# A written list of 1453 jobs in another order: linear attention, then a gated feed-forward block, on one core

## The chip, the core and the metric

The kernel runs on one core of one Trainium2 chip. It is written for the engines directly: TensorE (PE in the profile, with its weight loads as PEld), VectorE (DVE), ScalarE (ACT), GpSimd (POOL) and SyncE (SP). Each engine takes its own instructions strictly in the order in which the program issues them. SyncE does nothing but start DMAs here; GpSimd starts the loads from memory and most stores. The metric is the time of one execution on the device, in microseconds (us).

## What is computed

Inputs are q, k and v (8 batches, 8 heads, 576 positions, 64 values a head) and three weight matrices. First comes linear attention with position weights, then a feed-forward block over the 4608 tokens:

```python
r = np.maximum(x, 0.0); phi = concat([r * cos_w, r * sin_w])      # x = q, k
kv = einsum('bhsf,bhsd->bhfd', phi(k), v);  z = sum(phi(k), axis=2)
num = phi(q) @ kv;  den = phi(q) . z + 1e-6
x = (num / den)                        # 4608 tokens x 512
g = x @ w_gate;  val = x @ w_val       # 512 -> 1536
out = (silu(g) * val) @ w_out          # 1536 -> 512
```

The output is 4608 x 512 in float32.

## The kernel before, in words

The 4608 tokens are 36 tiles of 128, taken in nine groups of four tiles (group 0 to 8, `tg` in the code; a tile is `t`, a batch is `b`, and a batch has four and a half tiles). The kernel keeps three kinds of work going at once: attention for coming tiles, the two wide products of the current group, and the output product of the group before.

**Attention.** For each batch, GpSimd loads k, v and q (`load_job`, lines 120 and 125). ScalarE and VectorE make the features of q (`feature_jobs`, L880 to L890, into `r_q`), and SyncE transposes them by one DMA (L852, `phit<-r_q`). TensorE makes the key-value sums of a batch in 72 products of 64 rows (`kv_job`, L718); four copies bring them to memory (L630, tile `kv`). A tile's products (`tile_jobs`, L784 and L789) read both; then come the denominators (L803), the reciprocal (L809) and the multiplication to x (L817, L820). From tile 8 on SyncE turns x by a DMA (`turn_job`, L749, `xT<-x`); tiles 4 to 7 are turned by TensorE (L757) and copied by ScalarE (L630). For tiles 4 to 8 the features are turned by TensorE as well (`turned_tiles`, L1323), with a relu (L280, L282) and a multiplication (L1339).

**The wide products.** Group 0 and part of the value products are plain products of 512 columns (L440, L917, L1065). The rest goes through a scheme with seven products of half size, M1 to M7, in place of eight (`block_jobs`, L990), of 256 columns each, with sums of x (`x_sum_jobs`, L963) and of weights (L501) made ahead, and with copies and additions between the products (L630 on ScalarE, L1010, L1018 and L1026 on VectorE). A SiLU (L1049) and a multiplication (L1085) follow, and the result lies in `ht`.

**The output product** has the same scheme, P1 to P7 (`out_jobs`, L1155), with sums of `ht` (L1106), additions (L1198, L1212) and copies to the output buffer (L632, L636). Two output buffers take turns. Stores of group 0 go out on SyncE (L1124), those of groups 1 to 6 and half of group 7 on GpSimd, the other half of group 7 on SyncE. The last group uses buffers of its own, works in halves and stores in pieces on SyncE and ScalarE (L1253 for two tiles, L1262 for one).

**What sets the order.** All this work after the first 26.9 us is cut into 1453 jobs: one job is one instruction of VectorE or ScalarE, or the four to 72 products that belong together. A job knows what it must come after. At the end of the function stands `ORDER`, a list written out by number. The loop below it takes the words one after another and issues each job to its engine; so the list fixes, for every engine, the order of its instructions. A word is the job's number, then `a` or `v` where a job can run on either engine and is given to ScalarE or VectorE, and after a colon the numbers of the PSUM banks or buffer slots that the job takes:

```python
for word in ORDER.split():
    n, e, at = re.match(r"(\d+)([av]?):?([\d,]*)", word).groups()
    j, at = jobs[int(n)], [int(x) for x in (at.split(",") if "," in at else at)]
    j.eng = {"a": "ACT", "v": "DVE", "": next(iter(j.engs))}[e]
```

An engine whose next instruction isn't ready waits, and all that is listed behind it on that engine waits too, ready or not.

The numbers that matter below:

| jobs | what they are |
|---|---|
| 34; 35 to 38 | key-value job of batch 1; its four copies |
| 67, 84, 101 | turned features of tiles 4 and 5, 6 and 7, 8; relus 68, 70, 85, 87, 102 |
| 72, 78, 89, 95, 104 | products of tiles 4 to 8; their turns on TensorE (tiles 4 to 7) 76, 82, 93, 99; the copies of the turned x 77, 83, 94, 100 |
| 113 to 123; 124 | features of batch 2 (113 and 114 on VectorE, 115 to 123 on ScalarE); their transpose on SyncE |
| 55, 58, 61, 64; 56, 57, 59, 60, 62, 63, 65, 66 | copies of group 0's output; its stores |
| 182 to 185; 197, 199 | the four x sums of group 1; its products M7 and M6 that read 182 and 184 |
| 106, 107; 108 | tile 8's reciprocal and multiplication; its transpose |
| 142, 147, 152; 146, 151, 156 | products of tiles 9, 10, 11; the transposes of their x |
| 138; 139 to 141 | GpSimd's wait for tile 8's transpose; three loads behind it |
| 348; 354 | the first x sum of group 2; the product that reads it |
| 468 to 471, 474 to 477; 656; 657 | stores of group 2; GpSimd's wait for batch 4's features; a load |
| 523; 635; 710 | key-value job of batch 5; a copy of group 3's output to a buffer; a product of group 4 |
| 1307; 1309 to 1312 | the last product of group 7; the stores behind it on SyncE |
| 1422 and 1423; 1424 and 1425; 1427; 1431 and 1432 | last group: P6 in halves; the additions behind it; second part of P2; P5 in halves |
| 1410, 1414 | last group: two sums of `ht` for P3 |
| 1429, 1435; 1441, 1443, 1449, 1451 | last group: SyncE's stores of two tiles; its stores of one tile |

Of the kernel before, what the change touches and what calls it, by code (L numbers as in the profile page):

```python
# [18 lines left out]
def kernel(  # L19
# [1403 lines left out]
    for tg in range(1, NTG):  # L1423
# [43 lines left out]
        6:7 4:6 12:1 8:0 10:5 16:3 20:4 29 5:8 9:7 13:0 17:1 1:3 376 7 187 28 191 11 186 188 189 31 30 24:7 18:2 26:3  # L1467
        22:6 21:6 25:2 33 32 2:7 67:0 34:45 14:1 70a 36a 35a 38a 37a 3 27 380 19 68v 69 15 23 71 0 41:2 44 40:0 43
        72:340 84:7 78:561 39:1 42 73 74 75:3 85a 79 86 80 87v 81:2 88 76:3 77 45 101:7 89:560 95:341 47 90 96 377
        102a 378 91 92:3 97 48 82:5 93:6 55:1 83 94 98:0 192 193 109 190 103 110 113 381 114 46 99:1 51:3 52 49  # L1470
# [105 lines left out]
```

## Time and profile before

| | |
|---|---|
| three runs | 298.09, 299.3 and 299.79 us, median 299.3 |
| profiled execution | 298.66 us |
| its span, first to last instruction | 296.8 us |
| granted TensorE clock, mean | 0.996 |
| instructions | 8157, of them 3292 matmuls |
| DMA | 40.90 MB, mean 138 GB/s over the span |

The profile is of one execution, by the hardware's profiler. Its page gives the busy time of each engine, groups of instructions by line of the code with the mean duration of one and the idle time before them, and the chain of work that ended last. The trace behind it answers by stretch, by tile and by time. Matmuls overlap and their ends are modelled: the step from one product's start to the next one's says more than the length of either. A DMA's row on its queue is the time of its issue; when it landed is given apart.

### The profile page before, as it was taken

How to read it: one execution, taken by the hardware profiler on the slowest of the kernel's cores; microseconds unless marked ns; L12 is line 12 of the kernel's file. 1: busy time of each engine (PE TensorE's matmuls, PEld its weight loads, DVE VectorE, ACT ScalarE, POOL GpSimd, SP SyncE). 2: the span in 40 equal slices, each digit the busy share in tenths (PEclk: the TensorE clock that was granted, in tenths of full speed). 3: DMA queues.
4: the chain of work that ended last, by engine and by line, in shares of the span. 5: the costliest groups of instructions: out<-in, count | busy, mean ns of one | idle time of the engine just before them, and what ended most of it. 6: DMA issues, size and time to landing. Idle time of an engine off the chain costs nothing.

```text
span 296.8 us, 8157 instructions
## 1 busy us (share of the span) xinstructions
PE 290.1 (98%) x3292; PEld 237.7 (80%) x3292; DVE 252.9 (85%) x513; ACT 199.1 (67%) x423; POOL 69.1 (23%) x122
## 2 busy tenths in 40 slices
PE   8999999999999999999999999999999999999993
PEld 4697455665877888988898898888988898888882
DVE  7976889889987899999898977998778968968882
ACT  6664347978479868985499689976566555564630
POOL 7963530012015012213343020400050032002000
PEclk9999999999999999999999999999999999999998
DMA  7999999999969999599959947980270036000226
GB/s 255 232 196 198 202 206 209 229 202 155 170 149 171 199 209 144 102 172 148 209 118 159 197 68 131 208 146 2 38 171 8 2 89 127 0 2 18 55 53 161
DMA packets 71973, 40.90 MB, mean 138 GB/s; under 512 B 48768, under 2 KB 68736, under 8 KB 71936
## 3 DMA queue, kind: packets, MB, share of 16 engines
q0 software_dynamic: 24800, 24.39, 49.9%
q1 hardware_dynamic: 46528, 15.47, 27.6%
q10 hardware_dynamic: 608, 0.52, 0.6%
q8 instruction: 26, 0.43, 0.6%
q14 instruction: 11, 0.09, 0.1%
HBM read 37.75 MB, written 9.44 MB: 159 GB/s over the span
## 4 chain that ended last, share of the span: by engine, by line
PE 87%; DMA 9%; DVE 2%; issue 0%; DVEq 0%
PE banks L990 43%; PE banks L1155 23%; DMA xT<-x 4%; DMA phit<-r_q 4%; PE banks L440 4%; PE banks L917 4%; PE banks L1275 3%; PE banks L789 3%; PE banks L718 2%; PE banks L1065 2%; DMA wo_sb<-in_v_dram 1%; DVE v L292 1%; PE banks L371 1%; PE banks L784 1%; PE banks L1323 0%; PE banks L314 0%
## 5 line engine op out<-in xcount | busy, mean ns | idle before, releaser
L1124 POOL DMA_DIRECT2D out_dram<-ob x52 | 27.3, 532 | 128.4 <-ACT ob L632 87.6
L630 ACT COPY banks<-banks 128x512 f32<-128x512 f32 (+1 forms) x53 | 30.4, 577 | 22.3 <-PE banks L990 9.9
L1049 ACT ACTIVATE sg<-banks 128x512 bf16<-128x512 f32 x72 | 40.9, 599 | 5.8 <-PE banks L990 5.6
L1085 DVE TENSOR_TENSOR ht<-sg,banks 128x512 f16<-128x512 bf16 x60 | 40.4, 682 | 4.8 <-PE banks L990 4.4
L1155 PEld LDWEIGHTS <-ht 128*128 128x128 f16 x384 | 37.5, 98 | 4.5
L990 PEld LDWEIGHTS <-wg_sb 128*128 128x128 f16 x384 | 36.7, 98 | 5.3
L990 PEld LDWEIGHTS <-wgs_sb 128*128 128x128 f16 x368 | 35.4, 98 | 6.4 <-issue 0.5
L1010 DVE TENSOR_TENSOR banks<-m,banks 128x512 f32<-128x512 f32 x44 | 30.2, 692 | 7.3 <-PE banks L990 6.0
L990 PEld LDWEIGHTS <-wv_sb 128*128 128x128 f16 x320 | 31.2, 98 | 3.7
L990 PE MATMUL banks<-kvt,wgs_sb 128*128 128x256 f16 x236 | 33.8, 273 | 0.3 <-DVE kvt L963 0.3
L1155 PEld LDWEIGHTS <-sums 128*128 128x128 f16 x288 | 28.0, 98 | 3.4
L630 ACT COPY m<-banks 128x512 f32<-128x512 f32 x44 | 25.5, 590 | 5.7 <-PE banks L990 5.7
L990 PE MATMUL banks<-xT,wg_sb 128*128 128x256 f16 x192 | 28.6, 273 | 0.0
L632 ACT ACTIVATE ob<-banks 128x512 f32<-128x512 f32 x32 | 19.1, 596 | 10.6 <-PE banks L1155 9.3
L1155 PE MATMUL banks<-wo_sb,ht 128*128 128x256 f16 x192 | 25.2, 273 | 0.0
L990 PE MATMUL banks<-kvt,wg_sb 128*128 128x256 f16 x168 | 24.4, 273 | 0.0
L1155 PE MATMUL banks<-wt_sb,sums 128*128 128x256 f16 x192 | 24.2, 273 | 0.0
L820 DVE TENSOR_TENSOR x<-banks,rec 128x512 f16<-128x512 f32 x31 | 21.3, 690 | 3.1 <-PE banks L990 0.5
L990 PE MATMUL banks<-xT,wv_sb 128*128 128x256 f16 x160 | 23.8, 273 | 0.0
L1155 PE MATMUL banks<-wt_sb,ht 128*128 128x256 f16 x192 | 22.8, 272 | 0.0
L890 ACT ACTIVATE r_q<-raw_q,tanq 128x256 bf16<-128x256 bf16 x45 | 20.1, 507 | 0.0
L292 DVE TENSOR_TENSOR v<-raw_kv,tab 128x1152 bf16<-128x1152 bf16 x27 | 19.9, 750 | 0.0
(160 smaller groups left out, 540.1 us busy)
## 6 DMA issues: line engine op xcount, KB each, us to landing
out_dram<-ob POOLq DMA_DIRECT2D x52, 128.0 KB, 3.3
raw_kv<-in_k_dram POOLq DMA_DIRECT2D x7, 576.0 KB, 6.2
raw_q<-in_q_dram POOLq DMA_DIRECT2D x12, 288.0 KB, 9.9
raw_kv<-in_v_dram POOLq DMA_DIRECT2D x6, 576.0 KB, 9.3
out_dram<-ob SPq DMA_DIRECT2D x12, 128.0 KB, 2.8
wg_sb<-in_moe_w_gate_dram POOLq DMA_DIRECT2D x5, 256.0 KB, 9.0
wv_sb<-in_moe_w_val_dram POOLq DMA_DIRECT2D x5, 256.0 KB, 9.6
wo_sb<-in_v_dram SPq DMA_DIRECT2D x2, 576.0 KB, 4.1
```

The costliest lines, as they stand in the source:

```text
L292: nc.vector.tensor_tensor(out=v2s[b == 1][:, g, :, :, 0:D], in0=(first if b == 0 and g == 0 else {"v": raw_of(b, "v")})["v"][:, g].unsquee ...
L440: nc.tensor.matmul(out=st["f", tg, fc, lo][i], lhsT=(wg_sb, wv_sb)[i][:, kc, fs], rhs=xT[tg][:, ts, kc], start=(kc == 0), stop=(kc == KC - 1))
L630: nc.scalar.copy(out=out, in_=in_)
L632: nc.scalar.mul(out=out, in_=in_, mul=mul)
L820: tt(out=x_.rearrange("p (i y d) -> p i y d" if pairs else "p (y e d) -> p e y d", d=D, **({"i": 2} if pairs else {"e": 2})), in0=view()[: ...
L890: nc.scalar.activation(out=home()[:, :, c, 1], in_=raws[b, "q"][:, :, c], func=AF.Relu, scale=tanq[:, c:c + 1])
L990: nc.tensor.matmul(out=to[:, i], lhsT=a[:, c, 2 * u + i], rhs=x()[:, :, c], start=first and i == 0 and c == 0, stop=c == KH - 1, skip_grou ...
L1010: tt(out=bank(c), in0=one(m7_all, m).rearrange("p i x -> p (i x)"), in1=bank(b), op=ALU.add)
L1049: nc.scalar.activation(out=gates(rooms[w])[:, :, jh * HT:(jh + 1) * HT], in_=src, func=AF.Silu, scale=DOWN)
L1085: tt(out=ht[:, 4 * u + w:4 * u + w + 3:2, jh * HT:(jh + 1) * HT], in0=gates(rooms[w])[:, :, jh * HT:(jh + 1) * HT], in1=src.rearrange("p ( ...
L1124: {"POOL": nc.gpsimd, "SP": nc.sync, "ACT": nc.scalar}[j.eng].dma_start(out=out_v[idx // NC, idx % NC][:, cols], in_=ob_of(t)[e * SH:(e + ...
L1155: nc.tensor.matmul(out=to, lhsT=a[:, kc, i * P:(i + 1) * P], rhs=b[:, kc], start=first and kc == 0 and i == 0, stop=kc == HC - 1, skip_gro ...
```

## The change

`ORDER` is replaced by another list of the same jobs. Each job occurs once in both. TensorE's order differs in 379 of 490 places, GpSimd's in 51 of 74, SyncE's in 22 of 52; on VectorE and ScalarE nearly all places differ by some steps. 353 words name other banks or slots. Jobs 35, 37, 70, 85 and 102 go from ScalarE to VectorE, 68 and 87 from VectorE to ScalarE. No other line of the kernel changes. The parts of both lists that the text speaks of, shortened:

```diff
-        6:7 4:6 12:1 8:0 10:5 16:3 20:4 29 5:8 9:7 13:0 17:1 1:3 376 7 187 28 191 11 186 188 189 31 30 24:7 18:2 26:3
-        22:6 21:6 25:2 33 32 2:7 67:0 34:45 14:1 70a 36a 35a 38a 37a 3 27 380 19 68v 69 15 23 71 0 41:2 44 40:0 43
-        72:340 84:7 78:561 39:1 42 73 74 75:3 85a 79 86 80 87v 81:2 88 76:3 77 45 101:7 89:560 95:341 47 90 96 377
...
-        104:451 195:7 50 100 122 118 120 123 58 116 117 119 115 121 105 196:0 57 59 56 60 124 382 182 183 184 185 106
-        107:3 218:1 53 197:6 54 199 61:0 198:0 200:2 194 132 220:5 214:4 202 203 128 126 130 64 219:6 125 221:2 131
...
-        1424:1 1425:2 1430 1431 1432 1433 1434 1437 1438 1435 1436 1439 1445 1442 1440 1446 1444 1447 1441 1443 1449
-        1450 1448 1451 1452
+        4:2 8:5 6:4 10:3 12:0 5:2 9:1 13:0 376 7 1:3 11 187 20:4 16:6 24:7 14:1 2:5 22:3 26:2 21:8 29 25:3 188 189 191
+        30 31 3 33 32 28 0 27 15 67:7 34:45 40:1 39:0 42 18:2 68a 69 186 35v 37v 70v 23 71 36a 17:7 38a 19 377 84:5
+        78:341 72:670 43 41:2 44 79 87a 73 85v 80 380 378 86 74 81:0 75:1 47 45 89:341 101:5 76:6 90 88 91 92:3 102v
...
+        52 53 54 94 123 116 117 121 119 118 122 115 120 100 105 58 61:0 196:1 56 124 183 182 106 107:2 184 185 132
...
+        1418:1 1391 1411 1406 1426 1308 1412 1309 1420 1413 1427 1310 1421:0 1410 1422 1311 1428:1 1414 1423 1312
+        1424:4 1430 1431 1429 1425:5 1432 1433 1437 1434 1438 1435 1436 1439 1445 1441 1442 1440 1446 1443 1444 1447
+        1449 1450 1448 1451 1452
```

SyncE's first jobs are 57 59 56 60 124 108 63 66 65 62 146 156 151 168 in the old list and 56 124 108 62 60 57 146 65 59 63 66 156 151 168 in the new one. GpSimd's jobs around 656 are 656 477 475 657 501 658 471 502 in the old list and 656 474 476 475 471 477 657 501 658 502 in the new one.

More of the change, by code (lines that the diff above doesn't have):

```diff
@@ L1466 @@
     ORDER = """
-        6:7 4:6 12:1 8:0 10:5 16:3 20:4 29 5:8 9:7 13:0 17:1 1:3 376 7 187 28 191 11 186 188 189 31 30 24:7 18:2 26:3
-        22:6 21:6 25:2 33 32 2:7 67:0 34:45 14:1 70a 36a 35a 38a 37a 3 27 380 19 68v 69 15 23 71 0 41:2 44 40:0 43
-        72:340 84:7 78:561 39:1 42 73 74 75:3 85a 79 86 80 87v 81:2 88 76:3 77 45 101:7 89:560 95:341 47 90 96 377
-        102a 378 91 92:3 97 48 82:5 93:6 55:1 83 94 98:0 192 193 109 190 103 110 113 381 114 46 99:1 51:3 52 49
[63 rows of a table removed]
+        4:2 8:5 6:4 10:3 12:0 5:2 9:1 13:0 376 7 1:3 11 187 20:4 16:6 24:7 14:1 2:5 22:3 26:2 21:8 29 25:3 188 189 191
+        30 31 3 33 32 28 0 27 15 67:7 34:45 40:1 39:0 42 18:2 68a 69 186 35v 37v 70v 23 71 36a 17:7 38a 19 377 84:5
+        78:341 72:670 43 41:2 44 79 87a 73 85v 80 380 378 86 74 81:0 75:1 47 45 89:341 101:5 76:6 90 88 91 92:3 102v
[64 rows of a table added]
     """
```

119 rows, old and new, of the table ORDER are left out of this document.

## The prediction

> **What bounds the kernel now.** I read the head of the page first, then the busy time by stretch, then the chain of waits with each engine's timeline at the two places where TensorE stands still.
>
> ```profile
> span 296.8 us, 8157 instructions
> PE 290.1 (98%) x3292; PEld 237.7 (80%) x3292; DVE 252.9 (85%) x513; ACT 199.1 (67%) x423; POOL 69.1 (23%) x122
> ```
>
> TensorE is busy for 98% of the span. That is no proof of a full engine, so the next view cuts the span at the two places without work (columns: stretch; its length; busy us and count of PE, weight loads, VectorE, ScalarE, GpSimd; clock; DMA).
>
> ```profile
> 26.88:63.80 36.92, 36.92 (x463) 21.44 (x461) 31.59 (x69) 24.42 (x53) 8.31 (x12) 1.00 1.28 213
> 63.80:64.80 1.00, 0.68 (x8) 0.37 (x6) 1.00 (x2) 1.00 (x2) 0.00 (x0) 1.00 0.19 26
> 64.80:82.00 17.20, 17.20 (x144) 12.43 (x145) 15.59 (x30) 11.46 (x26) 2.92 (x5) 1.00 1.13 169
> 82.00:82.60 0.60, 0.27 (x4) 0.09 (x2) 0.50 (x2) 0.00 (x0) 0.00 (x0) 1.00 1.27 289
> 82.60:291.85 209.25, 209.25 (x2352) 184.73 (x2351) 181.80 (x345) 146.31 (x309) 39.13 (x73) 1.00 0.62 111
> 291.85:296.80 4.95, 0.00 (x1) 0.00 (x0) 0.42 (x1) 0.00 (x0) 0.00 (x0) 0.79 0.61 158
> ```
>
> The list of jobs begins at 26.88 us. From there to 291.85, which is 265.0 us, TensorE is idle for 0.32 and 0.33 us, at a clock of 1.00. The steps from product to product say whether it is also full (first the chain of waits: start, length, count; then TensorE's timeline at the first gap):
>
> ```profile
> 27.05 9.50 PE banks L917 x44
> 137.04 1.17 PE banks L718 x68
> 152.25 12.23 PE banks L990 x112
> 241.18 15.28 PE banks L990 x140
> ```
>
> ```profile
> 63.87 0.60 PE L990 MATMUL banks<-kvt,wg_sb 128*128 128x256 f16 x4
> 64.78 0.69 PE L789 MATMUL banks<-kv,phit 128*128 128x65 bf16 x16 [0.32 <-DMA phit<-r_q]
> ```
>
> A product of 256 columns steps by 12.23 / 112 = 0.109 us early and 15.28 / 140 = 0.109 late, one of 512 by 9.50 / 44 = 0.216. The code has 1232 + 672 of the first kind (L990, L1155) and 160 of the second after 26.88: 1904 x 0.1092 + 160 x 0.216 = 242.5 us. The seven key-value jobs at 1.17, and the small products of tiles and turns, take most of the other 22.5. So the list runs at TensorE's own pace, and **the same jobs in any order hold at least about 264 us of it.** An order can give back only waits. Start to start, the first wait is 64.78 - 63.87 - 4 x 0.109 = 0.47 us, since a modelled end (0.60 for four steps of 0.109) hides 0.16 of it; the second, by the same, 0.33 + 0.16 = 0.49. What the sum leaves beside them is no idle time. I take it as fixed: the new list goes over to tile products 27 times, the old one 24 times.
>
> **The change, part by part.** Both lists hold the same 1453 jobs: 490 of TensorE, 74 of GpSimd, 52 of SyncE. Nothing is computed anew; order, banks and slots change, and seven jobs change engine. I call the *place* of a product 26.88 plus the steps of all products listed ahead of it. With work this dense, it says when TensorE gets there, apart from waits.
>
> *1. The transpose of batch 2's features (124), and tile 9 (142) that waits for it.*
>
> ```profile
> 53.56 11.17 DMA phit<-r_q
> 47.84 1.63 ACT L630 COPY xT<-banks 128x512 f16<-128x512 f16 x3
> 49.36 1.70 ACT L890 ACTIVATE r_q<-raw_q,tanq 128x256 bf16<-128x256 bf16 x4
> 50.97 0.58 ACT L632 ACTIVATE ob<-banks 128x512 f32<-128x512 f32 x1
> 51.45 2.09 ACT L890 ACTIVATE r_q<-raw_q,tanq 128x256 bf16<-128x256 bf16 x5
> ```
>
> Before, ScalarE does three copies of turned x (83, 94, 100), four features, a copy out (58) and five features, and 124 leaves at 53.56. The new list puts all nine features straight behind the second copy, which ended at 48.9: nine at 0.42 (1.70 / 4, 2.09 / 5) end at 52.7, and 124 leaves 0.9 us earlier. Three of the four stores that SyncE issued just ahead of it go behind it. At 11.17 it lands at 63.9. Tile 9's place is 63.39, against 63.81 before; with 0.5 lost by then, as before (64.78 less the wait of 0.5 against 63.81), it is due at 63.9: the wait goes. **-0.5** (from -0.5 to 0). What is late next is the third copy.
>
> *2. The third copy (100), and the x sums of group 1 (182 to 185).*
>
> ```profile
> 53.47 0.60 PE L990 MATMUL banks<-kvt,wgs_sb 128*128 128x256 f16 x4
> 52.00 0.75 DVE L963 TENSOR_TENSOR kvt<-xT 128x512 f16<-128x512 f16 x2
> 53.72 0.20 DVE L809 RECIPROCAL rec<-den 128x8 f32<-128x8 f32 x1
> 54.03 0.76 DVE L817 TENSOR_TENSOR x<-banks,rec 128x256 f16<-128x256 f32 x2
> ```
>
> Copy 100 now starts at 52.7 and ends at 53.2 (1.63 / 3 = 0.54 each), where it ended at 49.5. The first two sums need it and end at 53.2 + 0.75 = 53.95. Their product (197, the first row) started 0.39 behind its place of 53.08; its new place is 53.51, so it is due at 53.9: it just fits. Behind them VectorE now has tile 8's reciprocal and multiplication (0.20 + 0.76), then the sum for product 199: ready at about 55.45, due at 54.82 + 0.4 = 55.2. **+0.3** (0 to 0.8).
>
> *3. The transposes of x tiles 11 and 10 (156, 151), and the sums of group 2 behind them (348).*
>
> ```profile
> 61.33 1.19 SPq L749 DMA_TRANSPOSE xT<-x  x1
> 62.63 3.33 SPq L1124 DMA_DIRECT2D out_dram<-ob  x4
> 66.91 6.35 SPq L749 DMA_TRANSPOSE xT<-x  x3
> 69.92 12.09 DMA xT<-x
> 82.10 0.44 DVE kvt L963
> DVE kvt L963 <- DMA xT<-x: 1.0, 1, 1.0
> DMA to landing us min/median/max: 11.9/12.8/13.8
> ```
>
> Before, SyncE issues four stores ahead of the three transposes; the new list puts three stores ahead of the first and four more between it and the other two. The last row is of the q loads that GpSimd issues at 67.2 to 67.9: 13.8 later, at 81.7, the last lands, and the transposes land at 82.0. Both end when the shared traffic ends. The four stores (3.33) make 156 and 151 leave about 2.4 us later, the start being up to 0.9 earlier by part 1. If landing goes by the end of the traffic, which starts up to 0.9 earlier too, 348 starts at 81.1 to 82.0; if it goes by the issue, at 84.4. VectorE itself, by the sums of its jobs in the new list, reaches 348 at about 81, as before (it waited from 81.1). Product 354 has place 81.11 in both lists. I take the row's end, 82.0, so **0** (from -0.5 to +2.4).
>
> *4. GpSimd's queue.*
>
> ```profile
> 136.55 0.17 POOL L837 COPY hold<-phit 1x2 bf16<-1x2 bf16 x1 [8.16 <-DMA phit<-r_q]
> 137.01 1.04 POOL L1124 DMA_DIRECT2D out_dram<-ob  x2 [0.29 <-issue]
> out_dram<-ob POOLq DMA_DIRECT2D x52, 128.0 KB, 3.3
> ```
>
> After this hold the new list issues five stores instead of two, then the loads; those start 1.6 us later. The fourth (471) must land before group 3's copy 635 may write its buffer: 137.0 + 3 x 0.52 + 3.3 = 141.9, and 635 is due at about 139.97 + 2.1 = 142.1 (the key-value job of the chain's 137.04 row began at 136.97, four steps of 0.016 earlier, 2.0 behind its place of 134.95). It fits by 0.2: **+0.1** (0 to 0.8). Elsewhere moved stores keep microseconds.
>
> *5. The last group and its stores.*
>
> ```profile
> 285.85 1.03 DVE L1106 TENSOR_TENSOR sums<-ht,sums 128x1024 f16<-128x1024 f16 x2
> 286.01 1.47 PE L1155 MATMUL banks<-wt_sb,sums 128*128 128x256 f16 x12
> 287.52 0.43 DVE L1198 SCALAR_TENSOR_TENSOR banks<-r_q,banks 128x256 f32<-128x256 f32 x1 [0.15 <-PE banks L1155]
> 289.28 0.61 SPq L1124 DMA_DIRECT2D out_dram<-ob  x1
> 289.99 1.16 SPq L1253 DMA_DIRECT2D out_dram<-r_q  x1
> 291.24 3.17 SPq L1262 DMA_DIRECT2D out_dram<-r_q  x4
> ```
>
> Before, product 1427 (four steps, 0.44) lay between P6's second half (1423) and P5's first (1431); now it comes earlier. P6's first half takes six steps, 0.655; its addition (1424) starts 0.2 after it and takes 0.43. That is ready 1.29 after 1422's start, and 1431's place is 1.31 after it. It fits only if VectorE is done with the two sums of the first row, which the new list still has right ahead: **+0.1** (0 to 0.4). On SyncE, group 7's store 1311 stood at 289.28 in front of the two-tile store 1435; it now goes ahead of 1429, and 1435 can leave up to 0.3 earlier. The four small stores follow it in turn, and the last also waits for the last addition: **-0.15** (-0.3 to 0).
>
> *6. Work that changes engine.* Five small jobs go from ScalarE to VectorE and two the other way, all before 46 us: about 1.8 us more for VectorE, busy 31.59 of 36.92 there (86%). Followed along the new list, tiles 4 to 8 come in time by 0 to 0.7 us: **0** (0 to +1.8).
>
> *7. All other places.* For each product that waits for one VectorE or ScalarE job behind another product, I compared the new distance in places with that kind's shortest turnaround in the trace (0.8 to 0.9 us for a copy or addition of 512 columns). Of 477 such products ten fall within 0.1 us of it, against six before, and five are short by 0.02 to 0.03. The rest lies in queues that I can't add up in whole: **+0.4** (0 to 1.5).
>
> Sum: -0.5 + 0.3 + 0 + 0.1 + 0.1 - 0.15 + 0 + 0.4 = +0.25 us. The profiled execution took 298.66 us, 1.86 more than its span, and would take 298.9. The three runs have their median at 299.3, 0.64 above the profiled one, but one of them lies 0.57 below it; I put half of the 0.64 on top: **299.2 us**, no change that 0.5% (1.5 us, about what a measurement of this kernel tells from none) would show.
>
> **The rivals.**
>
> *Late transposes (slower).* Part 3's other end: the landing follows the issue. VectorE stands at 348 until 84.4, and all that is listed behind it with it; 354 starts 2.4 later than before: 299.2 + 2.4 = 301.6. It decides once 151 lands after 82.0. For it: VectorE already waits here for this very transfer. Against it: it landed with the loads, not a fixed time after its issue, and 354 has no earlier place than before. The Trainium skill (DMA: Bandwidth & Descriptors, Queues, rings and completion order) says that each DMA engine consumes one ring's descriptors in ring order and goes round robin between rings. By that rule SyncE's four stores are moved ahead of both transposes, while GpSimd's loads only share; by it the sum is this rival's, at most 2.4 more. No trace here has stores between transposes. Chance 0.15.
>
> *VectorE falls behind (slower).* Part 6's upper end: the 1.8 us added early are not hidden, and tiles 4 to 8, and with them the first turns and sums, come that late: 301.0. For it: VectorE is busy 15.59 of 17.20 us in the next stretch also. Against it: TensorE never waited for VectorE before 82. Chance 0.09.
>
> *Many small waits (slower).* Part 7 above its range, 0.4 us in each of the eight groups: 299.2 + 3.2 = 302.4 or more. Chance 0.05.
>
> *Faster.* Both 0.5 us waits go, the stores gain 0.3 and nothing is added: 299.2 - 0.25 - 1.3 = 297.6. More isn't in the list, by the steps above. The Trainium skill (Perfetto Trace Analysis, Identifying the Most-Contended Engine) judges headroom by the share of weight loads, not of matmuls; by it 80% would leave a fifth to win. The trace's even steps of 0.109 us speak against that. Chance 0.05.
>
> **How the numbers follow.** The forecast, waits moved about with nothing large lost, has 0.66. Slower by over 0.5% (above 300.8): 0.15 + 0.09 + 0.05, less 0.02 for prices that stay below it, 0.27. Faster (below 297.8): 0.05. Within: 0.68. The range goes from the faster rival's edge, 297.9, to the many waits, 302.4; about 0.06 lies above and 0.06 below.
>
> **What would show it.** In the new trace: 124 leaving at about 52.7 and no wait at tile 9; 348 starting at 82 or earlier, or at 84 if the first rival holds; the start of 354 against 82.58; the first sums of group 1 at 53.2; 1435 close behind 1434. TensorE's steps of 0.109 and its count stay. The prediction is wrong if TensorE's idle time after 26.88 exceeds 2 us at any one place, or if the end moves with no wait in it.

## The result, and the profile after

| | before | new list |
|---|---|---|
| median of 20 runs each | 298.95 us (298.01 to 299.94) | 299.86 us (298.29 to 301.13) |
| ratio, 95% interval | | 1.0032 (1.0017 to 1.0047) |
| profiled execution; its span | 298.66; 296.8 | 301.13; 299.3 |

The new list is slower by 0.3%, some 0.95 us. That is inside the 0.5% that the forecast called no change, but its sign is measured. The profiled execution of the new list is the slowest of its 20, 1.27 above the median, so its profile shows more than the median lost. The page's head:

```profile
span 299.3 us, 8169 instructions
PE 290.5 (97%) x3292; PEld 237.7 (79%) x3292; DVE 253.3 (85%) x516; ACT 198.1 (66%) x420; POOL 68.8 (23%) x122
```

Nothing in the shares tells the two lists apart. The busy time by stretch does, once it is cut at the places where TensorE stands (columns as in the prediction):

```profile
26.88:43.48 16.60, 16.49 (x215) 8.36 (x213) 12.83 (x32) 6.88 (x13) 8.30 (x12) 1.00 1.35 201
43.48:44.48 1.00, 0.17 (x2) 0.00 (x0) 1.00 (x5) 0.00 (x0) 0.00 (x0) 1.00 1.26 211
44.48:193.81 149.33, 149.25 (x1736) 122.73 (x1735) 135.00 (x260) 119.74 (x263) 31.38 (x58) 1.00 0.97 167
193.81:194.80 0.99, 0.17 (x2) 0.03 (x1) 0.99 (x3) 0.99 (x3) 0.00 (x0) 1.00 0.58 125
194.80:255.59 60.79, 60.79 (x668) 54.43 (x669) 49.15 (x94) 37.29 (x75) 8.32 (x16) 1.00 0.37 69
255.59:256.74 1.15, 0.17 (x2) 0.00 (x0) 1.15 (x4) 0.06 (x1) 0.00 (x0) 1.00 0.00 0
256.74:294.55 37.81, 37.81 (x344) 33.55 (x343) 30.92 (x57) 17.36 (x33) 2.08 (x4) 1.00 0.17 41
294.55:299.26 4.71, 0.00 (x0) 0.00 (x0) 0.42 (x1) 0.00 (x0) 0.00 (x0) 0.85 0.52 131
```

Between three waits of 1.00, 0.99 and 1.15 us, counted start to start, TensorE has no other wait over 0.25; the old list had two of about 0.5, at other places. TensorE's timeline names what ends them (the number in brackets is 0.17 less, the modelled end):

```profile
44.48 0.81 PE L1275 MATMUL banks<-wo_sb,ht 128*128 128x512 f16 x3 [0.83 <-DMA wo_sb<-in_moe_w_out_dram]
...
194.80 0.60 PE L990 MATMUL banks<-xT,wg_sb 128*128 128x256 f16 x4 [0.82 <-DMA xT<-x]
...
256.74 0.60 PE L990 MATMUL banks<-raw_kv,wgs_sb 128*128 128x256 f16 x4 [0.98 <-DVE ht L1085]
```

The first is product 47 (rows 4 to 7 of w_out). The second is 1041, the first product of group 6's block, which reads x tiles 24 and 25. The third is 1319 of group 8, and there the named releaser is only the last link. VectorE's timeline:

```profile
253.34 0.68 DVE L1018 TENSOR_TENSOR m<-m,banks 128x512 f32<-128x512 f32 x1
255.33 0.76 DVE L963 TENSOR_TENSOR raw_kv<-xT 128x512 f16<-128x512 f16 x2 [1.30 <-DMA xT<-x]
256.01 0.68 DVE L1085 TENSOR_TENSOR ht<-sg,banks 128x512 f16<-128x512 bf16 x1
```

The multiplication 1275 (L1085) frees the bank that 1319 takes. The last product that it needs (1270, started at 253.85) ended at 254.45. It started only at 256.01, because the new list puts two x sums (1314, 1313) ahead of it on VectorE, and these wait for x tile 35; in the old list only 1314 stands ahead of it. Product 1319 also reads the sum 1313, which ended at 256.09. With 1275 ahead of the sums it could have started at about 256.1 in this execution, so about 0.6 of the 1.15 goes with VectorE's order and 0.5 with the late tile itself (an estimate from these rows). All three waits end with a transfer, as the chain of waits has it (start, length from issue to landing):

```profile
31.64 12.80 DMA wo_sb<-in_moe_w_out_dram
187.28 7.38 DMA xT<-x
248.31 6.90 DMA xT<-x
```

In the old list the two transposes landed in time: 841 (tile 24) at 187.39, where it now lands at 194.67, and 1184 (tile 35) at 250.96, now 255.21. SyncE's row of the four transposes of group 6, before and after, and the old list's TensorE at 1041, without a wait:

```profile
182.92 5.32 SPq L749 DMA_TRANSPOSE xT<-x  x4
```

```profile
183.16 7.63 SPq L749 DMA_TRANSPOSE xT<-x  x4
```

```profile
193.34 0.60 PE L990 MATMUL banks<-xT,vsums 128*128 128x256 f16 x4
193.77 0.60 PE L990 MATMUL banks<-xT,wg_sb 128*128 128x256 f16 x4
```

At the places of the prediction's parts 1 and 3 TensorE does not wait. It runs through tile 9 (142, at 65.28), and SyncE's transposes (53.66 features, 67.06 tile 9, 71.02 tiles 11 and 10 behind four stores) still come in time, since VectorE reaches 348 at 82.21 without a wait:

```profile
64.84 0.60 PE L990 MATMUL banks<-xT,wgs_sb 128*128 128x256 f16 x4
65.28 0.42 PE L789 MATMUL banks<-kv,phit 128*128 128x65 bf16 x8
```

```profile
53.66 6.90 SPq L852 DMA_TRANSPOSE phit<-r_q  x1
...
68.45 2.48 SPq L1124 DMA_DIRECT2D out_dram<-ob  x4
71.02 4.05 SPq L749 DMA_TRANSPOSE xT<-x  x2
```

```profile
81.61 0.68 DVE L1106 TENSOR_TENSOR sums<-ht,sums 128x1024 f16<-128x1024 f16 x1
82.21 0.75 DVE L963 TENSOR_TENSOR kvt<-xT 128x512 f16<-128x512 f16 x2
```

### The profile page after: what moved, and what is told of

It is laid out like the page before. It is cut to its first block, busy times and chain, and to the rows that moved or that the text cites. A ratio compares the mean times of both kernels' runs of the same rounds, so it can differ in the third digit from the quotient of the medians.

```text
span 299.3 us, 8169 instructions
## 1 busy us (share of the span) xinstructions
PE 290.5 (97%) x3292; PEld 237.7 (79%) x3292; DVE 253.3 (85%) x516; ACT 198.1 (66%) x420; POOL 68.8 (23%) x122
## 4 chain that ended last, share of the span: by engine, by line
PE 75%; DMA 17%; POOL 3%; DVE 2%; issue 1%; ACT 0%; SPq 0%; DVEq 0%; POOLq 0%
PE banks L990 39%; PE banks L1155 24%; DMA wg_sb<-in_moe_w_gate_dram 6%; DMA xT<-x 5%; PE banks L1065 5%; DMA wo_sb<-in_moe_w_out_dram 4%; PE banks L1275 3%; PE banks L789 2%; PE banks L718 2%; DMA wo_sb<-in_v_dram 1%; POOL wg_sb L268 1%; POOL wv_sb L269 1%; DVE ht L1085 1%; POOL raw_q L128 1%; DVE x L820 0%
## 5 line engine op out<-in xcount | busy, mean ns | idle before, releaser
L1049 ACT ACTIVATE sg<-banks 128x512 bf16<-128x512 f32 x72 | 42.1, 600 | 13.7 <-PE banks L990 13.5
L1085 DVE TENSOR_TENSOR ht<-sg,banks 128x512 f16<-128x512 bf16 x60 | 40.2, 680 | 2.3 <-ACT sg L1049 1.0
```

What stands on the lines that cost most here:

```text
L1049: nc.scalar.activation(out=gates(rooms[w])[:, :, jh * HT:(jh + 1) * HT], in_=src, func=AF.Silu, scale=DOWN)
L1085: tt(out=ht[:, 4 * u + w:4 * u + w + 3:2, jh * HT:(jh + 1) * HT], in0=gates(rooms[w])[:, :, jh * HT:(jh + 1) * HT], in1=src.rearrange("p ( ...
```

## The experiments

**Theory:** in the new list two transposes land after the products that need them are due, at 1041 and at 1319. **Rivals:** its first part costs the time (by 50 us this profile had lost 1.8 us, the old one's 0.3); or it is lost in many small places. "Slower" and "faster" are against the old list on the same chip; a ratio of 0.0010 is 0.30 us.

**Both late transposes repaired (w23).** SyncE's order of four transposes and VectorE's order of three jobs; nothing else moves (the diffs show the jobs of one engine by number, without their slots):

```diff
-851 846 856 841
+841 846 851 856
-1314 1313 1275
+1275 1313 1314
```

> The new list with two small moves: SyncE's transposes 841 and 846 of x tiles 24 and 25 go ahead of 851 (the order was 851 846 856 841), and on VectorE the multiplication 1275, whose input is ready at 254.5, goes ahead of the x sums 1313 and 1314, which wait for a transpose. Theory (late inputs): both waits, 1.0 at 1041 and 1.1 at 1319, go to at most 0.2, so this kernel is 1.6 to 2.1 us faster than the new list and 0.6 to 1.2 us faster than before; a wait at 47 of 0 to 1 stays. Rival (early stage): the waits move to the next products, or count little in the median, and the kernel stays within 0.5 us of the new list, slower than before. Rival (many small waits): 0.3 to 0.6 faster than the new list.

0.9996 (0.9985 to 1.0006): 1.1 us faster than the new list's ratio of 1.0032 (from another set of runs), and level with the old list. Both waits are gone. TensorE at the two places, then VectorE, where the multiplication now comes first:

```profile
193.24 0.60 PE L990 MATMUL banks<-xT,vsums 128*128 128x256 f16 x4
193.68 0.60 PE L990 MATMUL banks<-xT,wg_sb 128*128 128x256 f16 x4
```

```profile
253.43 0.69 DVE L1085 TENSOR_TENSOR ht<-sg,banks 128x512 f16<-128x512 bf16 x1 [0.53 <-PE banks L990]
254.03 0.75 DVE L963 TENSOR_TENSOR raw_kv<-xT 128x512 f16<-128x512 f16 x2
```

The step from 193.24 to 193.68 is four steps of 0.109: no wait. The gain against the new list is smaller than the 1.6 to 2.1 expected, and against the old list there is none. The theory had taken the waits of the slowest execution, the profiled one, for the median's. No wait over 0.25 us is left anywhere in this profile.

**The old list with one transpose moved (b841).** The reverse test of the first repair, in the old list:

```diff
-851 841 856 846
+851 856 846 841
```

> The old list with one move: SyncE's transpose 841 of x tile 24 goes from the second to the last of its four, as the new list has it (851 856 846 841). Theory (late inputs): it lands up to 1 us after product 1041 is due, in some executions and not in others (1.0, 0.7 and 0.0 in three profiles of lists with that order), so 0.3 to 0.9 us slower than before. Rival (the landing goes with the other traffic and not with the place among the four): within 0.2 us of before.

1.0029 (1.0015 to 1.0042): 0.87 us slower by one moved transfer. TensorE's timeline and the chain:

```profile
193.00 0.60 PE L990 MATMUL banks<-xT,vsums 128*128 128x256 f16 x4
194.54 0.60 PE L990 MATMUL banks<-xT,wg_sb 128*128 128x256 f16 x4 [0.94 <-DMA xT<-x]
```

```profile
187.86 6.54 DMA xT<-x
```

The step is 1.54 where 0.44 is full pace: 1.10 us at 1041. In the old list this move alone costs as much as the whole new list does. (The new list's order of the four, 851 846 856 841, differs from b841's by 846 and 856 as well.)

**The new list again, and each repair alone (a2, w2, w3).** w2 has the first two lines of w23's diff, w3 the last two.

> The new list itself once more, beside its two repairs on the same chip. Theory (two late transposes): it loses at 1041 and 1319 what the transposes 841 and 1184 come late in the execution at hand; so far 0.99, 0.70, 0.00 and 1.10 at 1041 where 841 is last, 1.15 and 0.80 at 1319. It gains nothing at tile 9 and at 354, since start of the list and waits to 85 us add up to 28.1 to 28.8 us in all profiles, the old list's too. So 0.5 to 1.4 us slower than before, and a profile whose own time is higher the longer these two waits are. Rival (the new list loses in many places): the same time, but with these two waits short the time stays over before by 0.5 or more.

> The new list with 841 and 846 ahead of 851 on SyncE, and nothing else moved. Theory (two late transposes): no wait at 1041, the one at 1319 stays at 0.5 to 1.2; 0.4 to 0.9 us faster than the new list, 0 to 0.8 slower than before. Rival (many places): within 0.3 us of the new list.

> The new list with the multiplication 1275 ahead of the x sums 1313 and 1314 on VectorE, and nothing else moved. Theory (two late transposes): no wait over 0.2 at 1319, the one at 1041 stays at 0 to 1.1; 0.3 to 0.9 us faster than the new list, 0 to 0.8 slower than before. Rival (many places): within 0.3 us of the new list.

| | ratio (interval) | wait at 1041 | wait at 1319 |
|---|---|---|---|
| a2, the new list | 1.0025 (1.0011 to 1.0038) | 1.18 | 1.44 |
| w2, 841 and 846 first | 1.0008 (0.9995 to 1.0020) | 0 | 0.89 |
| w3, 1275 first | 1.0000 (0.9989 to 1.0010) | 0 (841 still last) | 0.04 |
| w23, both | 0.9996 (0.9985 to 1.0006) | 0 | 0.04 |

```profile
194.21 0.60 PE L990 MATMUL banks<-xT,wg_sb 128*128 128x256 f16 x4 [1.01 <-DMA xT<-x]
...
256.43 0.60 PE L990 MATMUL banks<-raw_kv,wgs_sb 128*128 128x256 f16 x4 [1.28 <-DVE ht L1085]
```

These are a2's rows. Each repair gains 0.5 to 0.75 us on a2; their intervals do not tell the two apart. The repeat's profiled execution took 300.89, again the highest of its 12 (median 299.51), and it has both waits long. In w3's execution 841 was last too, but landed in time. The theory's size holds, the rival of many places does not: with the two repaired nothing over 0.25 is left, and on this chip a list with both repairs (best, below) is 0.84 us faster than a2.

How the loss divides is not shown. The two repairs alone add up to 1.26 us, more than a2 lost. And w3, which leaves 841 last, is as fast as the old list, while b841 lost 0.87 by that place alone.

**The first part of the list (ha, hb).** ha takes the new list's first 37 jobs and then the old list; hb the old list's first 53 jobs and then w23. The first products of ha:

```diff
-        6:7 4:6 12:1 8:0 10:5 16:3 20:4 29 5:8 9:7 13:0 17:1 1:3
+        4:2 8:5 6:4 10:3 12:0 5:2 9:1 13:0 376 7 1:3 11 187 20:4
...
```

> The new list for its first 37 jobs (to place 37 us, the plain products that begin it), then the old list. In five profiles of lists that begin as the new one, the start of the list and the waits to place 74 add up to 28.2 to 28.8 us; in the one profile of before to 27.9. Theory (the head varies by execution): what begins the list is paced by weights that land between 0 and 1 us apart from execution to execution, in either list; this kernel is within 0.3 us of before. Rival (the head is the list's own): the new first 37 jobs ask for weights in an order that costs 0.5 to 0.7 us; this kernel is that much slower than before.

> The old list for its first 53 jobs (to place 39.5 us), then the list w23 (the new list with 841 and 846 ahead of 851, and 1275 ahead of 1313 and 1314). Theory (the head varies by execution): within 0.3 us of w23, so 0 to 0.5 faster than before. Rival (the head is the list's own): the new head's 0.5 to 0.7 us are gone, so 0.6 to 1.0 us faster than before.

ha 1.0015 (0.9999 to 1.0031), hb 1.0007 (0.9996 to 1.0019). ha alone settles nothing: its interval holds both answers, and its profile has a wait of 1.02 at product 41, where the lists are joined, behind VectorE (`[0.85 <-DVE ht L937]`). hb falsifies the rival: with the old beginning, w23 gets no faster (0.3 us slower, within both intervals). Why becomes plain from the start of the list, whose code ahead of it is the same in all. The first product of the list in the old list, in b841 and in w23 starts at 26.89, 27.68 and 27.91; here b841 and w23:

```profile
27.68 1.03 PE L917 MATMUL banks<-xT,wv_sb 128*128 128x512 f16 x4
```

```profile
27.91 0.81 PE L917 MATMUL banks<-xT,wg_sb 128*128 128x512 f16 x3
```

A late start can take the place of early waits: with 27.91, w23 has no wait at 47; but s12 and a2, which start at 26.86 and 27.02, have none there either. Product 354 has place 81.11 in both lists. How far behind it TensorE starts 354 (late start and waits together), for nine lists with the new beginning or its middle: 1.89 (new list), 1.32 (s12), 1.51 (s123), 1.75 (w23), 1.66 (hb), 1.10 (a2), 1.46 (w2), 1.70 (w3) and 1.89 (best), mean 1.59; for lists that follow the old one from 39 to 85 us 1.47 (before), 1.62 (ha) and 1.19 (b841), mean 1.43. The lists of one kind differ among themselves by more than the two means do. So the wait of 1.00 at 47 was this execution's and not the list's, and the old list's two waits were its execution's: with the transposes in the same order, ha and b841 have 0.00 and 0.00 at 142, and 0.09 and 0.00 at 354.

**The features and the stores in the old list (bfeat).** Copy 58 behind the features, its stores behind 124, and stores put between the transposes (SyncE's order):

```diff
-57 59 56 60 124 108 63 66 65 62 146 156 151
+56 124 57 59 60 108 62 146 65 63 66 156 151
```

> The old list with ScalarE's copy 58 behind the features of batch 2 and its stores 57, 59 and 60 behind their transpose 124, and the stores 63, 65 and 66 behind the transpose 146, so that 156 and 151 stand behind three stores more. Theory: 124 leaves 0.5 to 0.6 earlier, the wait of 0.47 at tile 9 (142) goes, the transposes 156 and 151 land with the end of the shared traffic, and the wait of 0.5 at 354 goes or halves: 0.4 to 1.0 us faster than before. Rival (landing follows the issue): 354 waits 1 to 2 us more, 0.5 to 1.5 slower than before. Rival (both waits are filled by the next one): within 0.2 us of before.

1.0023 (1.0006 to 1.0041): slower by 0.7. 124 landed at 62.20 and 142 did not wait, but 354 waited 1.99. VectorE, TensorE and the chain:

```profile
83.33 0.76 DVE L963 TENSOR_TENSOR kvt<-xT 128x512 f16<-128x512 f16 x2 [1.43 <-DMA xT<-x]
```

```profile
83.81 0.93 PE L990 MATMUL banks<-kvt,wgs_sb 128*128 128x256 f16 x7 [1.83 <-DVE kvt L963]
```

```profile
71.59 11.65 DMA xT<-x
```

This is the size of the prediction's first rival, in the old list, but not its mechanism. What sets that landing can be read by comparing issue and landing over five executions (151 is the last transpose, 141 the last of the loads that GpSimd issues behind 108's landing):

| | 108 landed | 141 issued, landed | 151 issued, landed |
|---|---|---|---|
| before | 65.15 | 67.24, 81.73 | 69.92, 82.01 |
| b841 | 65.26 | 67.36, 81.44 | 70.37, 81.68 |
| new list | 63.09 | 65.19, 79.61 | 72.42, 80.78 |
| w3 | 63.19 | 65.29, 79.33 | 72.26, 80.34 |
| bfeat | 65.91 | 68.01, 82.82 | 71.59, 83.24 |

151 lands 0.2 to 1.2 us after the last load, whenever it was issued. The new list and w3, which share the order, issue it latest and have it earliest: 108 stands ahead of their stores, it lands 2 us earlier, and so the loads start 2 us earlier. bfeat has three stores ahead of 108. This fits the prediction's reading that the landing goes with the end of the shared traffic; no run moved the loads alone. The rule of ring order that the prediction cited (the Trainium skill, DMA: Bandwidth & Descriptors, Queues, rings and completion order) fits 108, which landed later with stores ahead of it; for 151 the stores cost about 1 us at most: it follows the last load by 1.0 to 2.0 us in the ten executions with four stores ahead of it, by 0.4 in bfeat with three, by 0.2 to 0.7 in the other three.

**New up to a place, then old (s1, s12, s123).** Three lists that change over at places 74, 197.6 and 285.

> The new list up to job 253 (place 74 us), then the old list; the same jobs, and every bank and slot stays as its list has it. Theory (late inputs): the new list wins the two old waits (tile 9's product 142 and product 354, 0.5 us each) and loses more at two later places, 1041 behind the transpose 841 (1.0) and 1319 behind the x sums 1314 and 1313 (1.15); the wait of 1.0 at product 47 belongs to the one profiled execution, because 47 was due at 43.48 there and 45 at 43.4 in the list before, while the load of w_out rows 4 to 7 landed at 44.44 in the one and 43.47 in the other. So this kernel is 0.5 to 1.0 us faster than before; no wait at 142 and 354, and a wait at 47 of anything from 0 to 1. Rival (early stage): the 1.5 us that the new list had lost more than the old one by 50 us are its own; then this kernel is 0.3 to 0.8 us slower than before, with a wait of about 1.0 at 47. Rival (many small waits over the whole list): within 0.2 us of before.

> The new list up to job 1046 (place 197.6 us), then the old list; one bank differs from both (job 1064 takes bank 4). Theory (late inputs): the kernel s1 and the wait of about 1.0 at product 1041 behind the last of four transposes, and small ones of 0.2: 0.8 to 1.3 us slower than s1, so 0 to 0.6 slower than before. Rival (early stage): nothing added to s1, within 0.3 us of it. Rival (many small waits): 0.4 to 0.6 slower than s1, with no single wait over 0.5 us.

> The new list up to job 1425 (place 285 us), then the old list, so only the very end is the old one's. Theory (late inputs): the kernel s12 and the wait of about 1.1 at product 1319 behind VectorE's x sums: 0.8 to 1.3 us slower than s12, 0.9 to 1.6 slower than before, and 0 to 0.3 slower than the whole new list, whose last stores leave earlier. Rival (early stage): within 0.3 us of s12. Rival (many small waits): 0.3 to 0.5 slower than s12.

| | ratio (interval) | single waits over 0.5 us |
|---|---|---|
| s1 | 1.0062 (1.0039 to 1.0085) | 2.14 (275, at 78.53) |
| s12 | 1.0056 (1.0041 to 1.0071) | 0.70 (1041), 1.61 (1000, at 204.26) |
| s123 | 1.0005 (0.9990 to 1.0020) | 0.80 (1319) |

As a division of the time these failed. s1 and s12 lose 3.8 and 1.6 us just behind the change of lists, where the one list's VectorE and ScalarE jobs do not match what the other has already done; s1's row at 78.53, and the stretch behind it (columns as in the prediction):

```profile
78.53 0.88 PE L1155 MATMUL banks<-wt_sb,sums 128*128 128x256 f16 x4 [1.97 <-DVE ht L1074]
```

```profile
78.50:82.20 3.70, 3.67 (x19) 2.65 (x19) 3.67 (x8) 0.60 (x1) 0.00 (x0) 0.54 1.27 236
```

Only 2.14 of s1's 3.8 us is a wait. Behind it the granted clock is 0.5 from 78.71 to 82.12, and the products of 256 columns step by 0.213 us in place of 0.109: this costs the other 1.7. None of the other executions has such a stretch inside the list, bfeat with its wait of 1.99 included.

Up to these places they are of use: s1's first 74 us have no wait at 47 or 142. s123 missed its expectation, being level with before. In its execution 841 landed at 192.30, and 1041 did not wait. It is the new list but for the order of the last 21 words, so its 1.0005 stands beside the new list's 1.0032 and 1.0025; the intervals overlap, and whether more than chance lies between them stays open.

**All repairs and four more moves (best).** w23 and:

```diff
-1174 1169 1179 1184
+1169 1179 1174 1184
-574 492
+492 574
-47 45 89 101
+101 47 45 89
-380 378 86 74 81 75 88
+86 74 81 75 88 380 378
```

> The list w23 with four more moves: the transposes 1169 and 1179 ahead of 1174 (their x tiles are ready 1 to 4 us earlier), the reading of the denominators 492 ahead of the copy 574 on ScalarE (the wait of 0.25 at 592 stands behind it), product 101 ahead of 47, and the weight sums 380 and 378 behind 88. Theory (the rest is TensorE's pace): w23 has no wait over 0.25 us left, so this kernel is 0.1 to 0.4 us faster than w23, 0.2 to 0.6 faster than before. Rival (the start is paced by landings): what is saved at the head comes back as a wait there, and the kernel is within 0.2 us of w23 and of before.

0.9997 (0.9982 to 1.0011): level with w23 and with before, as the rival said. It shows the landing side of 1319. SyncE's row, then GpSimd's stores of the same time in best, in the new list and in the old one:

```profile
239.07 6.28 SPq L749 DMA_TRANSPOSE xT<-x  x4
```

```profile
243.24 4.16 POOL L1124 DMA_DIRECT2D out_dram<-ob  x8 [22.38 <-ACT ob L632]
```

```profile
244.18 4.16 POOL L1124 DMA_DIRECT2D out_dram<-ob  x8 [22.37 <-ACT ob L632]
```

```profile
240.00 1.56 POOL L1124 DMA_DIRECT2D out_dram<-ob  x3 [19.22 <-ACT den L803]
243.96 2.60 POOL L1124 DMA_DIRECT2D out_dram<-ob  x5 [2.40 <-ACT ob L632]
```

In the old list three of the eight stores went ahead at 240.0, the transposes started at 241.3, and 1184 landed at 250.96. The new list issues all eight stores from 244.2 on and its transposes from 243.4 to 248.3 among them: 1184 landed at 255.21. In best three transposes go out before the stores, and 1184 landed at 249.21. That the stores delay it fits all three, but no run moved the stores alone.

## Why the prediction was right or wrong

The prediction was wrong: it forecast no change, and the time rose by 0.95 us, clear of the noise (the ratio's interval starts at 1.0017). 299.86 lies in the range and within 0.5%, but the sum of +0.25 came about by two terms that failed: part 7, the late inputs, was put at +0.4 and measured about 1.1, and part 1's gain of 0.5 isn't there. With what the runs showed for the seven parts (0, 0, 0, 0, +0.1, 0, +1.1) the sum would be +1.2.

1. **Part 1, -0.5:** the wait at tile 9 went, as said, but not by its reason, and the gain is not the list's: 124 left at 53.66 and not at 52.7, since TensorE, late by its wait at 47, had made ScalarE late (its nine features took 3.70 us, from 49.93), and landed 9.0 us after its issue. The landing of 11.17 us after issue was the longest among these executions; where the old list keeps that place (ha, b841), 124 landed 8.8 and 9.0 us after its issue and nothing waited. One execution's wait was priced as a property of the list. The same holds for the wait at 354. That 142 doesn't wait in the new list either is no gain over these.
2. **Part 2, +0.3:** not seen. The sums 182 and 183 ended in time, and neither 197 nor 199 waited in any of the executions.
3. **Part 3, 0:** right, by its own reason. 348 started at 82.21, and the transposes landed at 80.2 and 80.8, behind the loads. The rival's price was real in another order, by late loads: bfeat lost 1.99 at 354 with stores ahead of 108. Stores between transposes, which the prediction found in no trace, do stand in its own SyncE rows: four between 108 and 146.
4. **Part 4, +0.1:** 635 waited for TensorE's product until 142.90 and not for the store; 471 landed at 141.53, by the sum 141.9.
5. **Part 5, +0.1 and -0.15:** 1431 waited 0.10. 1435 left right behind 1434 (292.42 and 292.39). From TensorE's end to the span's end it is 4.71 in the new list and 5.04 in hb, which ends as it does, but with the old end 4.68 in ha, 4.72 in s123 and 4.94 in before: the gain is within what executions differ by.
6. **Part 6, 0:** right; no wait of TensorE for VectorE before 82 us in the new list's profile, and hb, with the old words of four of the seven jobs, is no faster.
7. **Part 7, +0.4: the step that failed.** It compared distances for products that wait for one VectorE or ScalarE job. It did not follow those that wait for a transfer (1041 for 841) nor an engine job that waits for one with a ready job behind it (1313 and 1314 ahead of 1275). That SyncE's four transposes of group 6 change order was in the list, and 841 from second to last is worth 0.87 in the old list (b841); the repairs of both places are worth 1.1 (w23) or, on one chip, 0.84 (best against a2). The range allowed for it, the likeliest value didn't.

Of the signs that it named for being wrong, "idle time after 26.88 exceeds 2 us at any one place" did not occur; the largest single wait in the new list was 1.15 us, in its repeat 1.44.

Open: why 841, last of the four, lands at 192.3 or 192.5 in some executions and at 193.8 to 194.7 in others, and so how often 1041 waits. Against product 1041, due at 193.0 to 193.8, this decides 0 or 1 us. GpSimd's stores beside it don't tell: their last landed at 191.6 to 192.3 in both kinds.

## What to carry to other kernels

In a full, hand-ordered list, check every transfer's last issue against its first reader, and every engine job that waits for a transfer against the ready jobs listed behind it; one transpose moved from second to fourth place cost 0.87 us in the old list here. Before a wait in one profile is booked as a gain, look whether it is there in a second execution: the old list's two waits were not. No list here gained by a wait removed before 85 us; what starts late or waits there varied more from execution to execution than from list to list.

## What was not expected of the hardware

The same code ahead of the list started it between 26.86 and 27.99 us, and by product 354 part of the difference was gone: s12 and w23 start 1.05 us apart and reach it 0.43 apart. After one wait of 2.14 us the granted clock was 0.5 for 3.41 us (s1), so the wait cost 3.8 us; one of 1.99 (bfeat) had no such stretch behind it. The last of four transposes issued back to back took 3.3 to 3.5 us on SyncE's queue in the new list's order (187.28 to 190.79), where the first three took 1.2 to 1.5, and landed 2.0 to 4.1 us after that. And a transfer issued 2.5 us later, behind four stores, landed 1.2 us earlier; the loads beside it had started and landed 2 us earlier.
